# A new written-out order for a linear-attention and token-mixing kernel on one core, from a plan in which small VectorE products exclude GpSimd and DMA transposes follow each other with more room

## The chip, the cores and the metric

The kernel runs on one core of a Trainium2 chip. A core has a matrix engine (TensorE, PE in the profile, with a queue of its own for loading weights, PEld), three engines for elementwise work (VectorE or DVE, ScalarE or ACT, GpSimd or POOL) and SyncE (SP), which here only starts DMA transfers. GpSimd can start transfers too, and does so for those that change the type. Each engine works through its own list of instructions in the order in which the program gives them; engines wait for each other through semaphores. The metric is the time of one execution on the device in microseconds (us); the median of several executions is the time of a kernel.

## What is computed

```python
# attention: B, H, S, D = 4, 8, 768, 48; state is D x D per batch and head
for t in range(S):
    cur = einsum('bhd,bhe->bhde', u * k[t], v[t])
    y[t] = einsum('bhd,bhde->bhe', r[t], state + cur)
    state = w * state + einsum('bhd,bhe->bhde', k[t], v[t])
x = y with its heads side by side                      # (4, 768, 384)
# mixing
theta = x @ w_theta
yr = einsum('ts,bsd->btd', w_tok_r, x * cos(theta))
yi = einsum('ts,bsd->btd', w_tok_i, x * sin(theta))
u = x + yr + yi
out = u + maximum(u @ w_ch, 0)
```

Inputs and output are float32; the kernel works in bfloat16 between.

## The kernel before

**Tiling.** The 768 steps of a batch are cut into chunks of 128, and two chunks make a pair: 3 pairs for each of 4 batches, 12 pairs, numbered 0 to 11. Pairs 0 to 6 take their loads with two neighbouring steps in one row; the later ones take chunks one behind the other. Within a chunk the recurrence becomes matrix products: K and R are multiplied by powers of the decay `w` (`Kw`, `Rw`, L552 and L554, on VectorE or GpSimd), transposed on TensorE against an identity (L491) and copied out of PSUM to `KT` and `RT` (L501 on ScalarE, L502 on VectorE). Scores are products of the two (L603), and VectorE multiplies them by a triangular 0/1 mask into `mAT` (L612). `PD` is the product of `RT` and `KT` (L619); from it comes a diagonal `dg` (L636, L641), which makes the bonus term `yd` with v in bfloat16, `vb` (L645; vb L579 to L583). The state is carried by the tiles `F`, `T`, `N`, `Sb`, `Sd` (L684 to L725). TensorE sums the outputs (L745 states, L758, L774 bonus, which uses the 0/1 tile `place`), and `x` is copied out (L782, L784).

For the mixing, x is transposed to `xT`, on TensorE for some pairs and by a DMA transpose for pairs 5 to 10; theta is a product (L833), cosine and sine run on ScalarE (L840, L844), and `z` is x times both (L848, VectorE). For each of the six chunk rows of a batch three mix tasks of four matmuls each (L870) sum over all 768 steps of a batch and so need the z of all its pairs. `un` adds x (L888, VectorE, into `uu_all`); it is transposed by a DMA transpose on SP's queue for all pairs but the last; the channel product (L903) reads the result; ScalarE applies the maximum (L910), GpSimd adds (L913), SP writes out (L930). The last two pairs end on VectorE (L918).

The mixing weights come by casting DMAs from GpSimd's queue into landing places in tiles that are not used yet (L460), are transposed on TensorE and copied out to `WrT` and `WiT`.

**Order.** All of this is recorded first as 746 tasks, in `P.add`, with what each reads and writes. A task has one way of being done, or several (which engine does it), each with an estimated cost in ns and a flag that says whether it keeps GpSimd from working at the same time. Nothing of these costs is used when the program is built: a planner outside the kernel used them, and left its result as five tables. `ORDER` lists the task numbers in the order in which they are issued, and so fixes the order of each engine's list; `WAYS` has one digit per task for the way; `BANKS` gives the PSUM banks in the order of their use; `AFTER` holds pairs (a, b) in which b is made to wait for a, beyond what the data demands; `IDLE` puts matmuls on a zero tile (fillers, into a bank that nobody reads) behind a task of TensorE: task, bank, number. Task numbers that matter below: 13 `thr` (three tiny operations, L344 to L348), 14 `mask` (L352), 15 `mask_c` (L356), 16 `place` (L361), 29 the small loads of w and u, 71, 114, 157 the Kw of pairs 0, 1, 2, 72, 115, 158 their Rw, 76 the copy of pair 0's RT, 84, 127, 170 the PD of pairs 0, 1, 2, 110, 153, 191 their z, 87 and 130 the yd of pairs 0 and 1, 120 the vb of pair 1, 60 a weight cast, 405 SP's load behind v of pair 1 (its place is read by 120), 355, 490, 506, 674 transposes of `un`.

SP's list at the start is k0, w, k1, r1, r0, the small w/u loads, v0, r2, k2, v1, and then the load that overwrites v1 and so waits for task 120.

Of the kernel before, what the change touches and what calls it, by code (L numbers as in the profile page):

```python
# [20 lines left out]
PE, DVE, ACT, POOL, SP = "PE", "DVE", "ACT", "POOL", "SP"  # L21
# [13 lines left out]


ORDER = [
# [39 lines left out]
]  # L77

WAYS = ("000000000000000000000000000000000000000000100001000010100100000010010000000010000000000000"
    "000001000000000000000000110000000000000000000000100000100000000000010000010000001000000000"  # L80
    "001010000000000010100000000000000010001000000000000000000001000020000000000001000100000000"
    "100000000000001000000000000000000000000000000000000000000000000000000000000000000000000000"
    "000000100001000000000000110010000001000000000000000010000000001000001010000000000000000000"
    "100000100000010000000000000000000000000000000000000000000000000000000000000000000000000010"
    "010000000001011001000000000000000000000100200000000000010000000000000000000001100002000000"
    "100100000000100000000000000000000000000000000000000000000000000000000000000000000000000000"
    "00000000000000000100001000")

BANKS = ("012345670123467523576034610573142716427403274167056732451734214526371675032145723041520715"
    "423527561407524163705701256372056240563513406142350674607534710524713601734654262645240376"  # L90
    "17641632540716306456324157063425176450317")

AFTER = [
# [5 lines left out]
]  # L99


IDLE = [
    (5, 1, 22), (7, 3, 10), (73, 4, 18), (75, 7, 18), (85, 7, 6), (78, 2, 4),
]


# [68 lines left out]
def kernel(  # L175
# [13 lines left out]
    nc = tc.nc  # L189
# [12 lines left out]
    P = Plan()  # L202
# [13 lines left out]
    place = sb.tile([C, 2, C], BF16, name="place")  # L216
# [3 lines left out]
    col_i = sb.tile([C, C], mybir.dt.int32, name="col_i")  # L220
    thr = sb.tile([C, 3], F32, name="thr")
    pi2 = sb.tile([C, 1], F32, name="pi2")
    wu = sb.tile([2 * HP, 2, Dp], F32, name="wu")
    tok_i = sb.tile([C, 1], mybir.dt.int32, name="tok_i")
    tok_f = sb.tile([C, 9], F32, name="tok_f")
# [68 lines left out]
    def setup():  # L294
        if WARM:
            P.add((DVE, 120, False, lambda: nc.vector.memset(zero, 0.0)), wr=["zero"],  # L296
                  prio=-3e4, name="zero")
        P.add((DVE, 250, False, lambda: nc.vector.memset(w_row, 0.0)), wr=["w_row"],
              prio=-2.9e4, name="w zero")
        P.add(sp(lambda: nc.sync.dma_start(out=w_row[:1], in_=rows_of(w, 1)), 400), wr=["w_row"],  # L300
              prio=-1e4, desc=(0, 1, 65), name="w_row", kind="small")
        P.add((DVE, 160, False, lambda: nc.vector.memset(ones, 1.0)), wr=["ones"], prio=-2.8e4,
              name="ones")
        P.add((DVE, 60, False, lambda: nc.vector.memset(pi2, math.pi / 2.0)), wr=["pi2"],
              prio=-210, name="pi2")
        if WARM:
            P.add(pe(WARM_NS[0], lambda: unread(P.bank_of["warm0"], WARM[0], 4)), rd=["zero"],
# [3 lines left out]
            rd=["w_row", "ones"], wr=["spread"], acq=["w"],  # L311
            prio=-1e4, mode=4, name="spread")
        if WARM:
            P.add(pe(WARM_NS[1], lambda: unread(P.bank_of["warm1"], WARM[1], 4)),
                  rd=["zero", "spread"], acq=["warm1"], prio=-1.1e3, name="warm")
# [5 lines left out]
              wr=["tok_i"], prio=-211, name="tok_i")  # L321
        P.add(pool(250, lambda: nc.gpsimd.iota(col_i, pattern=[[1, C]], base=0,
                                               channel_multiplier=0)),
              wr=["col_i"], prio=-210, name="col_i")
# [11 lines left out]
        def identities():  # L336
# [4 lines left out]
              name="ident")  # L341

        def thresholds():
# [2 lines left out]
            nc.vector.scalar_tensor_tensor(thr[:, :1], tok_f[:, 4:5], 2.0, thr[:, 2:],  # L346
                                           op0=Alu.mult, op1=Alu.add)
            return a, nc.vector.tensor_scalar_add(thr[:, 1:2], thr[:, :1], 1.0)  # L348
        P.add((DVE, 440, False, thresholds), rd=["tok_f"], wr=["thr"], prio=-203, name="thr")

        def masks():
            ins = [nc.vector.tensor_scalar(mask01[:, j], col_i, thr[:, j:j + 1], None,  # L352
                                           op0=Alu.is_gt) for j in range(2)]
            return tuple(ins)
        P.add((DVE, 400, False, masks), rd=["thr", "col_i"], wr=["mask"], prio=-201, name="mask")
        P.add((DVE, 200, False, lambda: nc.vector.tensor_scalar(  # L356
            mask_c, col_i, tok_f[:, 4:5], None, op0=Alu.is_gt)), rd=["tok_f", "col_i"],
            wr=["mask_c"], prio=-130, name="mask_c")

        def places():  # L360
            ins = [nc.vector.tensor_scalar(place[:, j], col_i, thr[:, j:j + 1], None,  # L361
                                           op0=Alu.is_equal) for j in range(2)]
            return tuple(ins)
        P.add((DVE, 400, False, places), rd=["thr", "col_i"], wr=["place"], prio=-140,
              name="place")
        P.add((DVE, 160, False, lambda: nc.vector.memset(wu, 0.5)), wr=["wu"], prio=-150,
              name="wu0")
# [606 lines left out]
```

## Time and profile before

| | us |
|---|---|
| median of three runs | 143.26 |
| lowest and highest | 142.03, 143.28 |
| the profiled execution | 142.16 |
| its span, first to last instruction | 140.4 |

| engine | busy us | share of the span |
|---|---|---|
| TensorE | 127.9 | 91% |
| VectorE | 110.9 | 79% |
| ScalarE | 76.1 | 54% |
| GpSimd | 75.0 | 53% |

The profile is one execution. Its views used below are: the busy time by stage; the timeline of an engine, whose rows give the start, the length, engine, line, operation, output and inputs, shapes, the count, and in square brackets the idle time before and what ended it; the chain of waits, followed back from the last instruction, with start and length of each piece; groups of equal instructions with busy time, mean ns of one, and idle time before them; and the table of who waited for whom. The span is first to last instruction, and the device time is a little longer. The granted TensorE clock was 0.994 of full speed.

### The profile page before, as it was taken

The page shows a single profiled execution, that of the slowest core. Times are in us where ns is not written, and L with a number is a line of the kernel's source. Part 1 is how long each engine was busy: PE and PEld are TensorE (multiplying, and loading weights), DVE is VectorE, ACT ScalarE, POOL GpSimd, SP SyncE. Part 2 cuts the span into 40 slices and gives each one's busy share as a digit, 9 for nine tenths or more (in the row PEclk, how much of TensorE's full clock was granted, in tenths as well). Part 3 has the DMA queues.
Part 4 walks back from the last instruction along what each step waited for, and adds up shares of the span by engine and source line. Part 5 has one row for each costly group of instructions (what it writes and reads, how often), then busy time and mean ns, then how long its engine had stood idle before and what let it go on. Part 6 is the DMA issues. An engine that isn't in the chain of part 4 may idle for free.

```text
span 140.4 us, 4622 instructions
## 1 busy us (share of the span) xinstructions
PE 127.9 (91%) x1937; PEld 86.6 (62%) x1937; DVE 110.9 (79%) x202; ACT 76.1 (54%) x149; POOL 75.0 (53%) x83
## 2 busy tenths in 40 slices
PE   5989588999999999979999999898999998999970
PEld 2757466776667776746566665665667775565630
DVE  7049999889889999988975899799689998254280
ACT  3077788598956695377765226751620738910200
POOL 5027669787074639509139966170668984800220
PEclk9999999999999999999999999999999999999997
DMA  4999599899999982799999799999999995432244
GB/s 103 268 257 260 82 204 147 191 244 221 240 278 234 283 190 20 127 161 164 270 249 198 146 181 130 254 155 176 244 215 287 114 99 141 158 117 56 56 168 168
DMA packets 67199, 25.47 MB, mean 181 GB/s; under 512 B 61801, under 2 KB 67178, under 8 KB 67178
## 3 DMA queue, kind: packets, MB, share of 16 engines
q1 hardware_dynamic: 64746, 22.23, 78.4%
q0 software_dynamic: 2432, 2.95, 13.4%
q8 instruction: 15, 0.25, 0.8%
q14 instruction: 6, 0.05, 0.2%
HBM read 20.06 MB, written 4.72 MB: 177 GB/s over the span
## 4 chain that ended last, share of the span: by engine, by line
PE 42%; DMA 24%; DVE 14%; POOL 11%; issue 3%; ACT 2%; SPq 1%; DVEq 0%; POOLq 0%; ACTq 0%
PE bank L870 21%; DMA uu_all<-uu_all 11%; PE bank L491 6%; DMA fin_all<-in_moe_w_tok_r_dram 5%; PE bank L903 5%; DMA ld<-in_r_dram 5%; PE bank L833 4%; DMA xT<-x 4%; DVE mAT L612 3%; POOL Kw L554 2%; DVE Rw L552 2%; POOL yd L645 2%; PE bank L603 2%; POOL PD L619 2%; DVE PD L619 2%
## 5 line engine op out<-in xcount | busy, mean ns | idle before, releaser
L870 PE MATMUL bank<-z,WrT 128*128 128x384 bf16 x144 | 46.9, 326 | 0.0
L870 PE MATMUL bank<-z,WiT 128*128 128x384 bf16 x144 | 46.8, 326 | 0.0
L913 POOL TENSOR_TENSOR fin_all<-fin_all,uu_all 128x384 f32<-128x384 f32 x20 | 17.9, 912 | 25.8 <-ACT fin_all L910 22.4
L888 DVE TENSOR_TENSOR uu_all<-bank,x 128x384 bf16<-128x384 f32 x24 | 12.9, 551 | 8.1 <-PE bank L870 6.6
L870 PEld LDWEIGHTS <-WrT 128*128 128x128 bf16 x144 | 14.1, 98 | 8.2 <-DVE z L848 0.3
L645 POOL TENSOR_TENSOR yd<-dg,vb 128x768 bf16<-128x768 f32 x10 | 14.7, 1472 | 7.8 <-DVE z L848 4.3
L870 PEld LDWEIGHTS <-WiT 128*128 128x128 bf16 x144 | 14.1, 98 | 7.6
L612 DVE TENSOR_TENSOR mAT<-bank,mask 128x512 bf16<-128x512 f32 x28 | 18.1, 680 | 0.3 <-PE bank L603 0.3
L910 ACT ACTIVATE fin_all<-bank 128x384 f32<-128x384 f32 x20 | 9.4, 492 | 16.3 <-issue 8.4
L903 PE MATMUL bank<-Wch,uu_all 128*128 128x384 bf16 x72 | 14.3, 326 | 2.4 <-DMA uu_all<-uu_all 2.4
L840 ACT ACTIVATE trig<-bank,pi 128x384 f16<-128x384 f32 x24 | 13.8, 590 | 3.4 <-PE bank L833 3.2
L501 ACT ACTIVATE RT<-bank 128x1024 bf16<-128x1024 bf16 x10 | 10.2, 1025 | 9.8 <-PE bank L491 9.7
L833 PE MATMUL bank<-Wth,xT 128*128 128x384 bf16 x72 | 14.5, 326 | 0.2 <-DMA xT<-x 0.2
L848 DVE TENSOR_TENSOR z<-x,trig 128x1536 bf16<-128x1536 bf16 x12 | 11.6, 965 | 3.1 <-ACT trig L844 3.0
L612 DVE TENSOR_TENSOR mAT<-bank,mask_c 128x512 bf16<-128x512 f32 x20 | 13.2, 680 | 0.4 <-PE bank L603 0.4
L844 ACT ACTIVATE trig<-bank 128x384 f16<-128x384 f32 x24 | 11.5, 497 | 2.0 <-PE bank L833 2.0
L289 PE MATMUL bank<-zero 128*128 128x128 bf16 (+1 forms) x92 | 10.3, 274 | 1.5 <-DVE zero L296 1.5
L552 POOL TENSOR_TENSOR Rw<-ld,rpow 128x768 bf16<-128x768 f32 x4 | 7.3, 1814 | 7.2 <-DVE z L848 6.3
L903 PEld LDWEIGHTS <-uu_all 128*128 128x128 bf16 x72 | 6.2, 97 | 7.1 <-DMA uu_all<-uu_all 3.4
L552 POOL TENSOR_TENSOR Kw<-ld,kpow 128x768 bf16<-128x768 f32 x3 | 5.4, 1809 | 9.4 <-DVE Kw L552 7.0
L603 PE MATMUL bank<-RT,KT 64*64 64x128 bf16 (+1 forms) x304 | 8.7, 219 | 1.8 <-DVE RT L502 1.3
L552 DVE TENSOR_TENSOR Rw<-ld,rpow 128x768 bf16<-128x768 f32 x8 | 9.2, 1152 | 1.4 <-DMA ld<-in_r_dram 1.4
(115 smaller groups left out, 232.0 us busy)
## 6 DMA issues: line engine op xcount, KB each, us to landing
ld<-in_r_dram SPq DMA_DIRECT2D x12, 384.0 KB, 5.8
out_dram<-fin_all SPq DMA_DIRECT2D x11, 384.0 KB, 2.8
ld<-in_k_dram SPq DMA_DIRECT2D x7, 384.0 KB, 4.9
ld<-in_v_dram SPq DMA_DIRECT2D x7, 384.0 KB, 7.0
ld<-in_k_dram SPq DMA_DIRECT2D x10, 192.0 KB, 4.7
ld<-in_v_dram SPq DMA_DIRECT2D x10, 192.0 KB, 5.6
fin_all<-in_moe_w_tok_i_dram POOLq DMA_DIRECT2D x1, 384.0 KB, 4.8
uu_all<-in_moe_w_tok_r_dram POOLq DMA_DIRECT2D x1, 384.0 KB, 5.8
```

The source lines that it names most:

```text
L552: return eng.tensor_mul(to.rearrange("p j h d -> p h j d")[:, :, :, :D], tokens(i), pw)
L603: ins.append(nc.tensor.matmul(to[:, hp * C:(hp + 1) * C], a, m, start=(hp == 0), stop=(hp == HP - 1), skip_group_check=True))
L612: mask01[:, j] if pairs else mask_c): nc.vector.tensor_mul(
L645: return eng.tensor_mul(yd.rearrange("p a b d -> p (a b) d"), wide(dg, D), vb.rearrange("p a b d -> p (a b) d"))
L833: ins = [nc.tensor.matmul(bank(th)[:, :HD], xT[:, t, dk, :], Wth[:, dk, :], start=(dk == 0), stop=(dk == ND - 1)) for dk in range(ND)]
L840: P.add(act(HD, lambda th=th, t=t, trig=trig: nc.scalar.activation(trig[:, t, 0], bank(th)[:, :HD], Act.Sin, bias=pi2), 144), use=[th], rd ...
L844: P.add(act(HD, lambda th=th, t=t, trig=trig: nc.scalar.activation(trig[:, t, 1], bank(th)[:, :HD], Act.Sin)), use=[th], rd=["sin"], wr=[( ...
L848: P.add(dve(4 * HD, lambda trig=trig, pr=pr: nc.vector.tensor_mul(z[:, 2 * pr:2 * pr + 2], bc(x[:, 2 * pr:2 * pr + 2], 2, 2), trig), 2.0, ...
L870: ins.append(nc.tensor.matmul(bank(tm)[:, :HD], (WrT, WiT)[ri][:, so, to * C:(to + 1) * C], z[:, so, ri], start=(part == 0 and i == 0), st ...
L888: P.add(dve(HD, lambda tm=tm, t=t, to=to, un=un: nc.vector.tensor_add(un[:, t], bank(tm)[:, :HD], x[:, to])), use=[tm], rd=[("x", xi, pr, ...
L903: ins = [nc.tensor.matmul(bank(tf)[:, :HD], uT[:, t, dk, :], Wch[:, dk, :], start=(dk == 0), stop=(dk == ND - 1)) for dk in range(ND)]
L913: P.add(pool(900, lambda t=t, un=un, fin=fin: nc.gpsimd.tensor_add(fin[:, t], fin[:, t], un[:, t])), rd=[("un", j, t)], wr=[("fin", j, t)] ...
```

## The change

Three things change. The planner's notes on five small VectorE tasks get the flag "excludes GpSimd" and other costs (these lines change nothing in the built program). The DMA transposes have more room in the plan; no line of the kernel shows that, and their number and their queue stay. And the tables `ORDER`, `WAYS`, `BANKS`, `AFTER` and `IDLE` are those of a new search.

```diff
 ORDER = [
-    1, 8, 10, 36, 17, 9, 20, 18, 0, 2, 19, 5, 111, 11, 21, 112, 12, 3, 37, 29, 6, 38, 7, 22, 155,
-    23, 24, 25, 154, 71, 26, 114, 73, 113, 74, 72, 116, 30, 117, 13, 115, 75, 31, 35, 77, 76, 28,
+    17, 8, 21, 36, 1, 3, 10, 2, 0, 18, 19, 20, 5, 37, 29, 9, 11, 12, 112, 13, 111, 38, 6, 154, 22,
+    30, 23, 7, 31, 24, 26, 155, 71, 25, 27, 16, 73, 72, 113, 74, 114, 75, 76, 14, 116, 35, 115, 32,
...
 AFTER = [
-    (71, 114), (72, 115), (127, 157), (163, 173), (110, 196), (191, 239), (238, 214), (238, 211),
...
-    (36, 45), (112, 50), (111, 55), (38, 65), (154, 70),
+    (14, 115), (158, 87), (158, 127), (170, 134), (170, 133), (163, 173), (191, 239), (238, 214),
...
+    (112, 39), (37, 40), (155, 45), (38, 50), (154, 60), (193, 65), (278, 70),
 ]
...
 IDLE = [
-    (5, 1, 22), (7, 3, 10), (73, 4, 18), (75, 7, 18), (85, 7, 6), (78, 2, 4),
+    (5, 1, 21), (6, 2, 6), (7, 4, 3), (73, 5, 12), (75, 6, 5), (116, 7, 5), (78, 4, 11),
+    (88, 6, 4), (124, 1, 3), (96, 7, 9), (107, 6, 7), (51, 6, 3),
 ]
...
-        P.add((DVE, 60, False, lambda: nc.vector.memset(pi2, math.pi / 2.0)), wr=["pi2"],
+        P.add((DVE, 60, True, lambda: nc.vector.memset(pi2, math.pi / 2.0)), wr=["pi2"],
...
-        P.add((DVE, 440, False, thresholds), rd=["tok_f"], wr=["thr"], prio=-203, name="thr")
+        P.add((DVE, 520, True, thresholds), rd=["tok_f"], wr=["thr"], prio=-203, name="thr")
...
-        P.add((DVE, 400, False, masks), rd=["thr", "col_i"], wr=["mask"], prio=-201, name="mask")
-        P.add((DVE, 200, False, lambda: nc.vector.tensor_scalar(
+        P.add((DVE, 470, True, masks), rd=["thr", "col_i"], wr=["mask"], prio=-201, name="mask")
+        P.add((DVE, 240, True, lambda: nc.vector.tensor_scalar(
...
-        P.add((DVE, 400, False, places), rd=["thr", "col_i"], wr=["place"], prio=-140,
+        P.add((DVE, 450, True, places), rd=["thr", "col_i"], wr=["place"], prio=-140,
```

What the new tables say where it matters below. On VectorE, `thr` stands right behind the identities, then Kw 0, place, Rw 0, Kw 1, mask. In all, 50 tasks go to another engine. Among those of the first 40 us: Kw of pairs 1 and 2, PD of pair 2, yd of pair 1 and Rw of pair 3 (196) go from GpSimd to VectorE; PD of pair 1 goes from VectorE to GpSimd; the copy of pair 0's RT goes from VectorE to ScalarE, and so do three of the weight copies (47, 52, 64), while two go the other way (59, 62). vb of pair 1 (120) stands on ScalarE behind pair 0's x copies, where it stood ahead of them. SP's list begins k0, w, r0, small w/u, r1, k1, v0, k2, r2, v1, and then the same load that waits for task 120. Rw of pair 2 (158) is now what releases GpSimd's yd of pair 0 and PD of pair 1; a weight cast (65) now waits for r of pair 3 (193). The fillers are 89 instead of 78. Behind transpose 490, TensorE's list has mix 500, mix 504, the transposes of R for pair 9 and an outer product more than before ahead of the first channel product that reads it; behind 674 one channel product more; behind 506 two mixes (686, 687) and a diagonal less, and a group of K transposes and a channel product more.

More of the change, by code (lines that the diff above doesn't have):

```diff
@@ L37 @@
 ORDER = [
[38 rows of a table removed]
[38 rows of a table added]
     724, 740, 727,
 ]
[L79 to L85, printed above, removed]
+WAYS = ("000000000000000000000000000000000000000000100000000000100101001000000000000000000000000000"
+    "000000000000000000000000010000000000010010011001000000100000000000000000010000000000000000"
+    "010010000000000000100000000000010011010000000000000000000001000020000001000000100100000010"
+    "000000000000101000000000000000000000000000000000000000000000000000000000000000000000000000"
+    "000000010000000000000010111000000001000000000000000000000000000000000011000000000000000000"
+    "110000200000010000000000000000000000000000000000000000000000000000000000000000000000000000"
+    "020000000001000010000000000000000000000100200000000000000000000000000000000001100002000000"
     "100100000000100000000000000000000000000000000000000000000000000000000000000000000000000000"
[L87 to L91, printed above, removed]
+    "00000000000000000100000000")
+BANKS = ("012345670134520642157630276145326437640516470627105426157321657635642561720436520514325073"
+    "514156714307142530617426137042137251376062501205713265726314652734105632761450146410416237"
+    "56367450261342507510735240735421736502413")
 AFTER = [
[5 rows of a table removed]
[6 rows of a table added]
 ]
 IDLE = [
-    (5, 1, 22), (7, 3, 10), (73, 4, 18), (75, 7, 18), (85, 7, 6), (78, 2, 4),
+    (5, 1, 21), (6, 2, 6), (7, 4, 3), (73, 5, 12), (75, 6, 5), (116, 7, 5), (78, 4, 11),
+    (88, 6, 4), (124, 1, 3), (96, 7, 9), (107, 6, 7), (51, 6, 3),
 ]
```

79 rows, old and new, of tables (AFTER, ORDER) are left out of this document.

## The prediction

> **What bounds the kernel now.** I read the page's first part, then busy times by stage, then the VectorE and GpSimd timelines of the start, the chain of waits, and last the single waits of TensorE.
>
> ```profile
> span 140.4 us, 4622 instructions
> PE 127.9 (91%) x1937; PEld 86.6 (62%) x1937; DVE 110.9 (79%) x202; ACT 76.1 (54%) x149; POOL 75.0 (53%) x83
> ```
>
> ```profile
> 0.00:37.00 37.00, 31.52 (x572) 22.84 (x573) 29.40 (x66) 25.69 (x48) 21.89 (x30) 1.00 0.98 200
> 37.00:118.00 81.00, 78.29 (x1253) 53.26 (x1251) 72.27 (x122) 44.86 (x91) 47.78 (x47) 1.00 1.05 189
> ```
>
> After its length, a stage row gives the busy time of TensorE, its weight loads, VectorE, ScalarE and GpSimd. From 37 to 118 us TensorE idles for 2.7 us of 81. What it does there is fixed, so a new order can win little more than those 2.7. In the first 37 us it idles for 5.5, and part of its busy time is filler on a zero tile. There VectorE is the full engine, and it is full of something else than work:
>
> ```profile
> 8.58 0.96 DVE L552 TENSOR_TENSOR Kw<-ld,kpow 128x768 bf16<-128x768 f32 x1 [5.11 <-ACT kpow L397]
> 9.75 2.51 DVE L552 TENSOR_TENSOR Rw<-ld,rpow 128x768 bf16<-128x768 f32 x1 [0.21 <-DMA ld<-in_r_dram]
> 12.18 0.14 DVE L344 TENSOR_SCALAR thr<-tok_f 128x1 f32<-128x1 f32 x1
> 12.35 1.81 DVE L346 SCALAR_TENSOR_TENSOR thr<-tok_f,thr 128x1 f32<-128x1 f32 x1
> ...
> 17.56 0.48 DVE L352 TENSOR_SCALAR mask<-col_i,thr 128x128 bf16<-128x128 int32 x2
> ...
> 21.82 1.49 DVE L361 TENSOR_SCALAR place<-col_i,thr 128x128 bf16<-128x128 int32 x2
> ```
>
> ```profile
> 9.62 1.81 POOL L552 TENSOR_TENSOR Kw<-ld,kpow 128x768 bf16<-128x768 f32 x1 [6.96 <-DVE Kw L552]
> 12.33 1.82 POOL L552 TENSOR_TENSOR Rw<-ld,rpow 128x768 bf16<-128x768 f32 x1 [0.89 <-DVE thr L344]
> ...
> 21.27 1.49 POOL L645 TENSOR_TENSOR yd<-dg,vb 128x768 bf16<-128x768 f32 x1
> ```
>
> Set the two fences side by side. VectorE's Rw (0.96 when alone, as Kw shows) takes 2.51 and ends 0.83 after GpSimd's Kw; a threshold on 128 numbers, 0.14 for its sister, takes 1.81 and ends with GpSimd's Rw; the two place products take 1.49 under GpSimd's yd, where the two alike mask products take 0.48. VectorE lost 1.55, 1.67 and 1.01 there: 4.2 us. It sits on the chain of waits (start, length):
>
> ```profile
> 14.21 0.63 PE bank L491 x8
> 14.84 1.22 DVE RT L502
> ...
> 16.10 0.40 PE bank L603 x14
> ...
> 29.31 7.39 DMA fin_all<-in_moe_w_tok_r_dram
> ...
> 37.59 1.30 PE bank L870 x8
> ...
> 69.46 0.49 PE bank L903 x3
> ```
>
> **The start, part by part.** The new order has the thresholds (task 13) done before any GpSimd product runs, and place (16) between Kw and Rw of pair 0. Pair 1's Kw (114) goes from GpSimd to VectorE, and GpSimd's Rw of pair 1 (115) gets an explicit wait for the masks (14). The chain: Kw to 9.54 as now (it waits for ScalarE's powers), place 0.5, Rw 0.96 to 11.0, transposes 0.63, the copy of RT on ScalarE instead of VectorE 1.03, scores near 12.75 instead of 16.10: 3.3 us sooner. Meanwhile VectorE does Kw 1 to 11.95 and the masks to 12.4. GpSimd's Rw 1 so runs from 12.4 to 14.2, as late as today. VectorE's PD product, ready at 13.9, has two inputs in SBUF as Rw has, and the row of 2.51 us says that it waits till 14.2. I take that 0.3; the ends are 0 and the 1.8 of a whole GpSimd product.
>
> The SBUF — State Buffer page of the Trainium skill, section "Who interferes with whom", has a rule that may speak against this part: a VectorE instruction with at most one SBUF input, outside the two-port modes, does not contend with GpSimd. If place is such a one, moving it is worth nothing by that rule, 1.0 us less than by the row, and the wait of 115 for 14 is pure loss. The row of place, 1.49 against 0.48, shows it waiting; the trace decides.
>
> How much of the 3.3 lives on?
>
> ```profile
> 31.57 0.96 DVE L848 TENSOR_TENSOR z<-x,trig 128x1536 bf16<-128x1536 bf16 x1
> ...
> 35.36 0.95 DVE L848 TENSOR_TENSOR z<-x,trig 128x1536 bf16<-128x1536 bf16 x1
> ...
> 38.51 0.95 DVE L848 TENSOR_TENSOR z<-x,trig 128x1536 bf16<-128x1536 bf16 x1
> ```
>
> ```profile
> L612 DVE TENSOR_TENSOR mAT<-bank,mask 128x512 bf16<-128x512 f32 x28 | 18.1, 680 | 0.3 <-PE bank L603 0.3
> L619 DVE TENSOR_TENSOR PD<-RT,KT 128x1024 bf16<-128x1024 bf16 x8 | 5.6, 696 | 0.1
> L645 DVE TENSOR_TENSOR yd<-dg,vb 128x768 bf16<-128x768 f32 x2 | 1.9, 944 | 0.0
> L502 DVE COPY WrT<-bank 128x768 bf16<-128x768 bf16 x4 | 2.2, 550 | 0.0
> L721 DVE TENSOR_TENSOR T<-bank,F 128x192 f32<-128x192 f32 x8 | 2.8, 350 | 0.2
> L840 ACT ACTIVATE trig<-bank,pi 128x384 f16<-128x384 f32 x24 | 13.8, 590 | 3.4 <-PE bank L833 3.2
> L844 ACT ACTIVATE trig<-bank 128x384 f16<-128x384 f32 x24 | 11.5, 497 | 2.0 <-PE bank L833 2.0
> L501 ACT ACTIVATE RT<-bank 128x1024 bf16<-128x1024 bf16 x10 | 10.2, 1025 | 9.8 <-PE bank L491 9.7
> L501 ACT ACTIVATE WiT<-bank 128x768 bf16<-128x768 bf16 x3 | 2.4, 815 | 0.2 <-PE bank L491 0.2
> L579 ACT ACTIVATE vb<-ld 128x768 bf16<-128x768 f32 x6 | 5.0, 838 | 0.0
> L782 ACT ACTIVATE x<-bank 128x384 bf16<-128x384 f32 x11 | 5.0, 495 | 4.9 <-PE bank L774 4.8
> ```
>
> Ahead of the first z product VectorE has, in the new order, 12 score masks of 0.68, 6 Kw or Rw of 0.96, 2 PD of 0.70, a yd of 0.94, 3 weight copies of 0.55, place, masks and uw (1.3 together), 5 state sums of 0.35, an x and a vb of about 0.55: 22 us. Each starts some 0.08 before its forerunner's end (12.18 against 9.75 + 2.51), which leaves 19. From 8.58 that is 28, and today's first z starts at 31.57. But two others are late next:
>
> ```profile
> SPq L446 <- ACT vb L579: 7.6, 1, 7.6
> ld<-in_r_dram SPq DMA_DIRECT2D x12, 384.0 KB, 5.8
> ```
>
> SP's next load waits 7.6 us for ScalarE's vb of pair 1, which now stands behind pair 0's x copies. VectorE reaches the end of Rw 2 near 17.8; that releases GpSimd's yd (1.49), then come the bonus matmuls (about 0.6) and two x copies: 20.9, and vb to 21.7 instead of 23.2. All loads behind it move up by some 1.4, no more. Pair 3's r, 5.8 us to landing, then holds its Rw, which the new order puts on VectorE ahead of z. And ScalarE takes over RT and weight copies; I get its cosines and sines of pair 0 to an end near 30.1 (31.3 today). So the first z comes at about 31.3, 0.3 sooner, with one group of transposes (0.63) more already done. Up to the second z ScalarE still has two sines, two cosines, two weight copies, an x and an RT, 5.3 us or some 4.9 overlapped: 35.0; the third comes near 37.8. The cast whose landing ends TensorE's wait at 36.7 goes out some 1.4 sooner, since GpSimd has lost work ahead of it; with that stall gone, pair 1's z is late in its place. **I take 1.0 us for the start**; the ends are 3.3 and a loss of 2.2 (ScalarE, below).
>
> On SP, r0 and the two small w/u loads pass r1 and k1. k1 isn't needed before 11.0 and today's fourth load is there by 9.75: free. The casts' new waits are for early loads, or for r of pair 3 while GpSimd is idle behind it: nothing. Eleven more fillers stand in gaps: nothing, or 0.7 where TensorE isn't idle:
>
> ```profile
> 10.13 1.17 PE L289 MATMUL bank<-zero 128*128 128x128 bf16 x18
> ```
>
> **The DMA transposes.** All still go through SP's one queue; their places and TensorE's work behind them change.
>
> ```profile
> 61.55 0.82 PE L903 MATMUL bank<-Wch,uu_all 128*128 128x384 bf16 x4 [0.71 <-DMA uu_all<-uu_all]
> ...
> 88.18 0.66 PE L903 MATMUL bank<-Wch,uu_all 128*128 128x384 bf16 x3 [0.68 <-DMA uu_all<-uu_all]
> ...
> 97.01 0.66 PE L903 MATMUL bank<-Wch,uu_all 128*128 128x384 bf16 x3 [0.55 <-DMA uu_all<-uu_all]
> ...
> 116.93 0.66 PE L903 MATMUL bank<-Wch,uu_all 128*128 128x384 bf16 x3 [0.49 <-DMA uu_all<-uu_all]
> ```
>
> For each I compared TensorE's tasks between the last mix that feeds the transpose and the first channel product that reads it. Turn 490 (88.18) gains two mixes of 0.65 (1.30 for two), a transposing group and more, 1.9 or over: its 0.68 goes. Turn 674 (116.93) gains a channel product, 0.49: its 0.49 about goes. Turn 506 (97.01) loses about 0.5 on balance: its wait stays or doubles. Turn 355 (61.55) hangs on a VectorE sum at the same place: stays. **I take 1.1 us**; the ends are 2.4 (all four) and a loss of 0.5. Past the start ScalarE's extra copies (7.5 us over the whole kernel, of 64 idle) are hidden: its rows idle for TensorE.
>
> **The sum.** The profiled execution took 142.16, 1.8 more than its span: 142.16 - 1.0 - 1.1 = 140.1. It lies 1.1 below the median of the runs, 143.26; the same 2.1 off the median is 141.2.
>
> **Rivals.** *All of the start lives on*: z near 28, loads in time. For it: VectorE was the full engine; against it: SP's 7.6 us. 143.26 - 3.3 - 1.1 = 138.9. *It doesn't do what it says*: collisions go, but the loads keep z where it was, and transposes on one queue land as before: 143.26 - 0.3 = 143.0. *ScalarE takes VectorE's place between 30 and 38 us*: up to the third z it gains RT, three weight copies and small ones against two weight copies and small ones, net 1.5; this decides if the second z starts later than 35.36. Then all mixing comes 1.5 later, and the 0.7 of fillers stands before work: 143.26 + 2.2 = 145.5. For it: it works in order and is busy 25.69 of 37; against it: that leaves 11 idle.
>
> **Chances.** Forecast 0.45, all of the start 0.14, nothing 0.18, ScalarE late 0.23. One per cent, 1.43 us, is about what a measurement of this kernel can tell from no change. The forecast's own range is 139.8 to 142.6; 0.34 of its 0.45 lies below 141.8. So faster 0.34 + 0.14 = 0.48, within 0.11 + 0.18 = 0.29, slower 0.23. The range 138.7 to 145.3 takes in the first rival and about half of the last.
>
> **What would show it.** Thresholds and place without a stretched one, no Rw of 2.5 us; scores of pair 0 near 12.8; the load behind ScalarE's vb near 21.7; z products near 31.3, 35.0 and 37.8; no channel product waiting near 88 and 117. A second z after 35.4, transposed K and R that wait for ScalarE while TensorE idles, or over 3 us of TensorE idle from 37 to 118 would make it wrong.

## The result and the profile after

| us | before | after |
|---|---|---|
| median, runs side by side on one chip | 142.06 | 140.38 |
| lowest and highest of 20 runs each | 140.63, 143.57 | 139.17, 142.53 |
| profiled execution, its span | 142.16, 140.4 | 140.2, 138.4 |

The ratio of after to before is 0.9878, 95% interval 0.9843 to 0.9913: faster by 1.2%. The prediction's 141.2 against the 143.26 that it started from is a ratio of 0.9856, inside that interval. The runs of one kernel spread by 2 to 3 us, so single profiles are read below for where time goes, and the repeated runs for how much. Ratios and their intervals, here and below, take in only those runs of a kernel that lie within 1.5% of its fastest, while the medians take in all, so a ratio isn't the quotient of two medians.

The page after, first the span and the busy time of each engine:

```profile
span 138.4 us, 4633 instructions
...
PE 129.0 (93%) x1948; PEld 87.6 (63%) x1948; DVE 106.6 (77%) x197; ACT 81.6 (59%) x158; POOL 70.1 (51%) x79
```

The two stages (length, then busy time of TensorE, weight loads, VectorE, ScalarE, GpSimd):

```profile
0.00:37.00 37.00, 33.33 (x592) 24.44 (x593) 28.41 (x69) 27.06 (x49) 15.42 (x27) 1.00 1.00 211
37.00:118.00 81.00, 79.59 (x1259) 53.89 (x1258) 70.53 (x116) 49.46 (x99) 49.82 (x47) 1.00 0.95 188
```

Between 37 and 118 us TensorE now idles for 1.4 us where it idled for 2.7. VectorE's busy time fell by 4.3 us over the whole kernel, ScalarE's rose by 5.5, GpSimd's fell by 4.9. The table of who waited for whom, TensorE's rows:

```profile
PE bank L291 <- DVE zero L298: 1.7, 1, 1.7
PE bank L835 <- issue: 1.2, 1, 1.2
PE bank L671 <- issue: 1.0, 1, 1.0
PE bank L493 <- DVE Kw L554: 0.3, 1, 0.3
```

There is no row for a channel product that waits for its DMA transpose. Before, the four waits shown with the prediction made the largest row, 2.4 us; now all four are gone, where the prediction counted on two. Two rows are new: TensorE stood still for 1.2 and 1.0 us, and "issue" says that nothing the profile records released it.

The start on VectorE, in order:

```profile
9.10 0.96 DVE L554 TENSOR_TENSOR Kw<-ld,kpow 128x768 bf16<-128x768 f32 x1 [1.02 <-ACT kpow L399]
9.97 0.48 DVE L363 TENSOR_SCALAR place<-col_i,thr 128x128 bf16<-128x128 int32 x2
10.36 0.95 DVE L554 TENSOR_TENSOR Rw<-ld,rpow 128x768 bf16<-128x768 f32 x1
11.23 0.95 DVE L554 TENSOR_TENSOR Kw<-ld,kpow 128x768 bf16<-128x768 f32 x1
12.10 0.48 DVE L354 TENSOR_SCALAR mask<-col_i,thr 128x128 bf16<-128x128 int32 x2
...
14.23 0.87 DVE L621 TENSOR_TENSOR PD<-RT,KT 128x1024 bf16<-128x1024 bf16 x1
```

Rw takes 0.95 where it took 2.51, and the two place products 0.48 where they took 1.49: these collisions with GpSimd are gone, as the prediction took them from the old rows. The rule weighed there (the Trainium skill, "SBUF — State Buffer", section "Who interferes with whom") would have left place as slow as it was, if place is a product outside the two-port modes; it got 1.0 us quicker for two. Whether it runs in such a mode no run here shows. The scores of pair 0 follow on TensorE at 13.15 us, 2.95 sooner than before (16.10). The three z products:

```profile
32.02 0.95 DVE L850 TENSOR_TENSOR z<-x,trig 128x1536 bf16<-128x1536 bf16 x1
...
34.77 0.95 DVE L850 TENSOR_TENSOR z<-x,trig 128x1536 bf16<-128x1536 bf16 x1
...
37.97 0.95 DVE L850 TENSOR_TENSOR z<-x,trig 128x1536 bf16<-128x1536 bf16 x1
```

They stand 0.45 later, 0.59 and 0.54 sooner than before. So nearly 3 us of lead at 13 us have become half a microsecond at 35, and the span ends 2.0 sooner: most of the time must be won elsewhere. Half a microsecond is little to read from single profiles: in the other profiles of kernels with the old start unchanged, the first z stands anywhere from 30.79 to 31.62 us.

### The profile page after: what moved, and what is told of

It is laid out like the page before. It is cut to its first block, busy times and chain, and to the rows that moved or that the text cites. A ratio compares the mean times of both kernels' runs of the same rounds, so it can differ in the third digit from the quotient of the medians.

```text
span 138.4 us, 4633 instructions
## 1 busy us (share of the span) xinstructions
PE 129.0 (93%) x1948; PEld 87.6 (63%) x1948; DVE 106.6 (77%) x197; ACT 81.6 (59%) x158; POOL 70.1 (51%) x79
## 3 DMA queue, kind: packets, MB, share of 16 engines
q0 software_dynamic: 2432, 2.95, 13.0%
## 4 chain that ended last, share of the span: by engine, by line
PE 75%; DVE 9%; ACT 4%; DMA 3%; issue 3%; POOL 1%; SPq 1%; DVEq 0%; POOLq 0%
PE bank L872 29%; PE bank L493 10%; PE bank L835 8%; PE bank L905 7%; PE bank L291 4%; PE bank L605 4%; DMA ld<-in_r_dram 3%; PE bank L671 3%; PE bank L760 2%; DVE Rw L554 2%; PE bank L812 2%; PE bank L776 2%; PE bank L638 2%; DVE mAT L614 1%; POOL Rw L554 1%
## 5 line engine op out<-in xcount | busy, mean ns | idle before, releaser
L554 POOL TENSOR_TENSOR Rw<-ld,rpow 128x768 bf16<-128x768 f32 x6 | 10.9, 1816 | 18.3 <-DVE mask L354 10.1
L291 PE MATMUL bank<-zero 128*128 128x128 bf16 (+1 forms) x103 | 12.3, 275 | 1.7 <-DVE zero L298 1.7
L503 ACT ACTIVATE RT<-bank 128x1024 bf16<-128x1024 bf16 x12 | 12.4, 1030 | 2.1 <-PE bank L493 2.0
L291 PEld LDWEIGHTS <-zero 128*128 128x128 bf16 x103 | 8.0, 111 | 5.0 <-issue 1.9
L503 ACT ACTIVATE KT<-bank 128x1024 bf16<-128x1024 bf16 x9 | 9.2, 1021 | 2.8 <-PE bank L493 2.8
L647 POOL TENSOR_TENSOR yd<-dg,vb 128x768 bf16<-128x768 f32 x7 | 10.3, 1475 | 0.8 <-DVE Rw L554 0.6
L554 DVE TENSOR_TENSOR Rw<-ld,rpow 128x768 bf16<-128x768 f32 x6 | 7.6, 1261 | 2.2 <-DMA ld<-in_r_dram 2.2
```

The costliest lines, as they stand in the source:

```text
L291: ins = [nc.tensor.matmul(bank_t[k][:, :wide * C].rearrange("p (a c) -> p a c", a=wide), zero, bc(zero, 1, wide), start=True, stop=True, s ...
L503: P.add([act(n * C, lambda: nc.scalar.activation(dst, src(), Act.Copy)), dve(n * C, lambda: nc.vector.tensor_copy(dst, src()), 1.0 if pair ...
L554: return eng.tensor_mul(to.rearrange("p j h d -> p h j d")[:, :, :, :D], tokens(i), pw)
```

## The experiments

Two theories stood at the beginning. By theory A the gain is shared as the prediction had it, 1.0 us in the start and 1.1 at the transposes; by theory B all of it is won behind 36 us. In all the kernels the whole computation is left in; only tables differ. "New" and "old" in the short diffs are the tables after and before. A kernel made of the two takes the first tasks of one order and then all the rest in the sequence of the other; each task keeps the engine that it has in the order it is taken from, and the waits of `AFTER` go with it.

**The start alone, and the rest alone.**

```diff
-ORDER = old
+ORDER = new[:186] + [s for s in old if s not in new[:186]]   # new up to 36 us
```

> The first 186 tasks of the changed order (up to about 36 us), the rest in the old order. Theory A (the prediction's split: start 1.0, transposes 1.1): 1.0 us faster than the kernel before, ratio 0.993. Theory B (the start's lead, 2.7 us at 15 us in the changed trace, is used up by the first z product, and the whole gain comes from the channel products that no longer wait for DMA transposes): within 0.4 us of before, ratio 0.997 to 1.003, and the four waits of 0.5 to 0.7 us of channel products are back.

```diff
-ORDER = old
+ORDER = old[:186] + [s for s in new if s not in old[:186]]   # new from 36 us on
```

> The first 186 tasks in the old order, the rest in the changed one. Theory A: about 1.0 us faster than before, ratio 0.993. Theory B: the whole gain of the change, 1.7 us, ratio 0.988, with the three Rw, threshold and place stalls of VectorE (4.2 us) still there and no channel product waiting.

The start alone gave 0.9969 (0.9923 to 1.0016), the rest alone 0.9878 (0.9838 to 0.9919). The rest by itself is worth what the whole change is worth, as theory B has it. Its stage row, and TensorE's two largest waits in it, both of the first 13 us:

```profile
37.00:118.00 81.00, 80.35 (x1262) 54.28 (x1262) 70.86 (x117) 50.05 (x100) 51.36 (x48) 1.00 1.00 189
```

```profile
PE bank L283 <- DVE zero L290: 1.5, 1, 1.5
PE bank L485 <- POOL Kw L546: 1.0, 1, 1.0
```

From 37 to 118 us TensorE idles for 0.65 us: the four waits on transposes are gone, and nothing stands in their place. One thing in it was not as expected: of the three stalls of VectorE in the old start the first, at Rw, isn't there in this profile (0.96 us, not 2.51), and its first z stands at 30.79 us, 0.78 sooner than in the kernel before with the same order. So a part of this profile's lead isn't the rest's, and only its waits are read. The start alone kept one of them (0.6 us), and got two of 0.7 us on the transposes of x.

**Only later channel products.** The kernel before, with six channel products one to three TensorE tasks later, so that the transposes have time to land.

```diff
-ORDER = old
+ORDER = old with 356 and 359 behind 376, 491 behind 504, 507 behind 478, 675 and 678 behind 691
```

> The kernel before, in which only the channel products that waited for a DMA transpose stand one to three TensorE tasks later (six of them). Theory B, if cover behind the transposes is all it needs: the four waits (2.4 us in all) go and the kernel is 1.5 to 2.4 us faster, ratio 0.983 to 0.989. Rival: what stands behind them waits in their place (z products or VectorE sums are the next to be late): under 0.5 us faster, ratio over 0.996.

1.0028 (0.9993 to 1.0063): no gain. The four waits are gone, and others stand in TensorE's table:

```profile
PE bank L826 <- DMA xT<-x: 1.3, 1, 1.3
...
PE bank L484 <- DMA z<-in_moe_w_tok_i_dram: 0.7, 1, 0.7
PE bank L484 <- ACT fin_all L903: 0.6, 1, 0.6
```

TensorE comes to other tasks whose data are not there either: a transpose of x (1.35 us, at 99.06) and ScalarE's step behind a channel product that is now later (0.58, at 64.33), 1.9 us where 2.4 went. The wait for a weight cast, 0.7, is at 39.62 us, ahead of everything that was moved, and so belongs to this execution and not to the change. Room behind a transpose brings nothing here if everything else stays.

**The small products alone.** The kernel before, with thresholds, masks and place directly behind the identities, ahead of any GpSimd product.

```diff
 ORDER = [
-    ... 111, 11, 21, 112, 12, 3, 37, ...
+    ... 111, 11, 21, 112, 12, 13, 14, 16, 15, 3, 37, ...
```

> The kernel before, in which thresholds, masks, place and the causal mask stand right behind the identities on VectorE, where it idles for 5 us; nothing else is moved, the stretched Rw of 2.5 us stays. VectorE saves 4 us of blocked and own time in the start. Theory B (loads and ScalarE end the lead): scores of pair 0 earlier by about 1.9 us, but under 0.5 us faster in all, ratio over 0.996. Rival (VectorE sets the start): 1.5 us faster or more, ratio under 0.990.

0.9966 (0.9923 to 1.0009). The scores of pair 0 stand at 14.19 us, 1.91 sooner, as expected; the time, as with the new start, is 0.3% less at the middle and not told from nothing.

**Where in the rest.** The new order from 63 us on, from 105 us on, and between the two only.

```diff
-ORDER = old
+ORDER = old[:343] + [s for s in new if s not in old[:343]]   # from 63 us on
+ORDER = old[:603] + [s for s in new if s not in old[:603]]   # from 105 us on
+ORDER = the first of these up to its 603rd task, then the sequence of old   # 63 to 105 us
```

> The kernel before up to about 63 us, the new order behind it. The old start with the new rest from 36 us on gave 0.9878. Theory C: the gain lies behind 63 us, at the transposes of 82 to 97 us and of 110 to 117 us whose channel products no longer wait (0.68, 0.55 and 0.49 us of wait in the kernel before, 1.7 us together): ratio 0.985 to 0.991, and no wait of a channel product on a transpose behind 63 us. Rival D, that the stretch from 36 to 63 us carries it (its lead there in one profile was the 0.8 us with which it came out of the start): ratio above 0.996.

> The kernel before up to about 105 us, the new order behind it. Theory C: only the last waiting transpose (0.49 us of wait) and the work around it are changed: ratio 0.994 to 0.998, 0.3 to 0.8 us. Rival D': the last third carries most: ratio below 0.992. Rival: nothing of it here: 0.999 to 1.002.

> The kernel before with the new order between about 63 and 105 us alone: two of the waiting transposes lie there (0.68 and 0.55 us of wait). Theory C: both waits are gone and the rest follows: ratio 0.989 to 0.994, 0.8 to 1.5 us. Rival: what is won there is waited for behind it, as with the channel products that were only put later: ratio 0.998 to 1.002. With the run from 105 us on this should add up to the run from 63 us on.

They gave 0.9947 (0.9901 to 0.9992), 1.0109 (1.0069 to 1.0150) and 1.0067 (1.0025 to 1.0109). The first is a smaller gain than was expected, the others are losses, and they do not add up: the expectations failed. The likely cause, not tested by itself, is the seam: at 105 us the two orders have different tasks done, and a kernel that changes over there must catch up. TensorE's longest waits, in the kernel from 105 us on and in the one between:

```profile
108.55 0.62 PE L484 MATMUL bank<-ident,Kw 128*128 128x128 bf16 x8 [1.23 <-DVE F L710]
```

```profile
108.61 0.62 PE L484 MATMUL bank<-ident,Rw 128*128 128x128 bf16 x8 [1.05 <-POOL Rw L545]
```

Both stand just behind the seam; neither whole kernel stops there. These runs so don't share the gain out over the stretches; that stays open.

**Less room in the new order.** The changed kernel with the transposes 490 and 506 behind the loads that stand next in SP's queue, with their channel products in place.

```diff
-ORDER = new
+ORDER = new with 490 behind 534 (load v), 506 behind 572 and 571 (loads of k)
```

> The changed kernel with two of its DMA transposes, those issued at 82.73 and 88.71 us, put behind the loads that stand next in SP's queue, so some 2.4 and 2.3 us later; their channel products at 88.45 and 94.11 us keep their places. Theory: room is what counts, and a wait of TensorE on a transpose is paid in full: about 1.5 us of wait at each comes back, and the time rises by 2 to 3 us, ratio to the kernel before 1.002 to 1.010. Rival: TensorE is behind other work anyway, and the waits take the place of others: 0.988 to 0.995.

1.0009 (0.9969 to 1.0050), 1.3% above the changed kernel's 0.9878: 1.9 us, below the 2 to 3 expected. Only one wait came back. SP's row of the second transpose and TensorE's row of the product that reads it:

```profile
89.32 1.46 SPq L503 DMA_TRANSPOSE uu_all<-uu_all  x1
```

```profile
94.55 1.15 PE L898 MATMUL bank<-Wch,uu_all 128*128 128x384 bf16 x6 [1.47 <-DMA uu_all<-uu_all]
```

The first transpose went out at 82.45 us (82.73 in the changed kernel), since the load ahead of it was quickly issued; its product stood 5.29 us behind it instead of 5.72, and didn't wait. The second cost a wait of 1.47 us, and it is paid; the rest of the 1.9 isn't accounted for. Room is needed, then, but by itself it brings nothing: the first half of that from this run, the second from the later channel products.

**Three products between the engines.** In the rest, tasks 366 (a Kw), 382 (a yd) and 422 (a PD) went from GpSimd to VectorE. Once they are put back in the kernel of old start and new rest, once moved alone in the kernel before.

```diff
-WAYS = old start, new rest
+WAYS = the same, with 366, 382, 422 on GpSimd
```

> Old start and new rest from 36 us on (0.9878 before), with the products 366, 382 and 422 of the rest put back from VectorE to GpSimd, where the kernel before had them (1.81 us, 1.47 us and 2.12 us there, 0.95, 0.95 and 0.83 us on VectorE). Theory F: these three are what lets the rest run ahead of the transposes, and the gain of 1.7 us falls to 0.5 us or less: ratio 0.996 to 1.003, with TensorE waiting for GpSimd near 60 or 75 us. Theory C: the order and the room behind the transposes carry the gain, the engine of three products does not: ratio 0.986 to 0.992.

```diff
-WAYS = old
+WAYS = old, with 366, 382, 422 on VectorE
```

> The kernel before, order and start unchanged, with the products 366, 382 and 422 alone put from GpSimd (1.81, 1.47 and 2.12 us) to VectorE (0.95, 0.95 and 0.83 us). Theory F1: the engine of the three is the gain by itself, whatever the order: ratio 0.985 to 0.992. Theory F2: engine and order only gain together, because in the old order TensorE waits for none of the three (its waits behind 36 us are the channel products' on the transposes): ratio 0.997 to 1.004, with the waits of the channel products still there.

Put back: 0.9987 (0.9945 to 1.0030), no gain left that can be told from nothing. Moved alone: 1.0151 (1.0096 to 1.0205), 1.5% slower, outside what either theory expected. (Both profiled executions lie 1.4 and 1.7 us above their kernel's median, so waits are read from them, not the total.) GpSimd's timeline in the first, and TensorE's row behind it:

```profile
73.77 2.12 POOL L613 TENSOR_TENSOR PD<-RT,KT 128x1024 bf16<-128x1024 bf16 x1 [0.20 <-ACT RT L495]
75.84 1.48 POOL L639 TENSOR_TENSOR yd<-dg,vb 128x768 bf16<-128x768 f32 x1
...
79.14 1.83 POOL L548 TENSOR_TENSOR Kw<-ld,kpow_c 128x768 bf16<-128x768 f32 x1
80.91 2.54 POOL L546 TENSOR_TENSOR Rw<-ld,rpow 128x768 bf16<-128x768 f32 x1
```

```profile
83.50 0.62 PE L485 MATMUL bank<-ident,Rw 128*128 128x128 bf16 x8 [1.21 <-POOL Rw L546]
```

PD and yd, 3.6 us of GpSimd, push the Kw and Rw behind them, and TensorE waits 1.21 us for that Rw. In the kernel before, VectorE made it, at 72.42 us; the new order gives it (task 451) to GpSimd, in exchange for PD and yd, so that this run undoes one half of an exchange. Task 366 makes TensorE wait in the same way near 57 us, for 0.52 us. The other run does one half of it alone. VectorE then has no good place for the PD:

```profile
78.44 1.74 DVE L612 TENSOR_TENSOR PD<-RT,KT 128x1024 bf16<-128x1024 bf16 x1
```

```profile
77.82 1.81 POOL L547 TENSOR_TENSOR Kw<-ld,kpow_c 128x768 bf16<-128x768 f32 x1
```

```profile
80.84 0.43 PE L662 MATMUL bank<-vb,Kw 128*64 128x48 bf16 x16 [1.05 <-DVE mAT L605]
```

It runs into GpSimd's Kw (to 79.63 us) and takes 1.74 instead of the 0.83 that it takes in the changed kernel, where GpSimd has nothing beside it but the last 0.28 us of a cast; the score mask behind it is late, and TensorE waits 1.05. A collision as in the old start comes back here. It isn't the largest wait of this profile: at 69.67 us TensorE waits 1.77 for a transposed x, and whether the three products are behind that too isn't shown. Nor were the waits moved along that hold GpSimd back in the new order: (366, 261), (366, 297), (382, 326) and (382, 329) of `AFTER`. So neither the order with these three on the old engine nor the engine with the old order has the gain: it needs both. Which of the other 30 tasks of the rest that change their engine matter, no run tried.

**No fillers.** The changed kernel without its 89 fillers, to see what the two "issue" gaps belong to.

```diff
-IDLE = [(5, 1, 21), (6, 2, 6), ... (51, 6, 3)]
+IDLE = []
```

> The changed kernel without its 89 filler matmuls, which compute nothing that is used. In two profiles of kernels with the new start TensorE stood still in front of its matmuls number 350 and 861 (1.02 and 1.19 us, and 1.30 and 0.49 us), and nothing that the profile shows released it. Theory E: the gaps belong to the place in TensorE's own list of instructions, not to the work there: without the fillers number 350 is other work, reached some 3 us later, so the gap of 1.0 us in the outer product near 22.3 us goes, any gap that is left stands in front of number 350 or 861 again, and the time falls by 0.5 to 1.5 us against the changed kernel: ratio to the kernel before 0.977 to 0.985. Rival: the gaps belong to the work (outer product, theta product): they stay there, ratio 0.986 to 0.990. Rival: the fillers are needed, the granted clock falls in the first 20 us and the time rises: above 0.995.

0.9867 (0.9786 to 0.9949): not told from the changed kernel, and not the gain of 0.5 to 1.5 us that was expected; its six runs spread from 139.17 to 143.86. The granted clock was 0.999 in the profiled execution, but 0.962 and 0.971 in two of the others, where the changed kernel with its fillers had 0.981 or more in 20 runs. Whether the fillers are needed for the clock stays open. The gap at 22 us is gone and the first z stands at 30.23 us instead of 32.02. But a longer gap appears elsewhere, at other work:

```profile
46.30 0.32 PE L863 MATMUL bank<-z,WrT 128*128 128x384 bf16 x1 [1.67 <-issue]
```

What that says is told in the last section.

**The best of both.** The old start with the small products early, and the new rest.

```diff
-ORDER = old
+ORDER = (old[:186] with 13, 14, 16, 15 behind 12) + [s for s in new if s not in old[:186]]
```

> Old start with the four small products of the set-up (thresholds, two masks, place) directly behind the identities, and the new rest from 36 us on. The two parts gave 0.9966 and 0.9878 by themselves. If they add: ratio 0.980 to 0.987, about 139.2 us. If what the start wins is waited for at the loads near 36 us, as in the changed kernel: 0.986 to 0.991.

0.9826 (0.9783 to 0.9869), a median of 139.18 us, with all its runs between 138.86 and 139.63. That fits two parts that add (0.9966 times 0.9878 is 0.9844). It is faster than the kernel before; against the changed kernel the intervals overlap, so that it is the faster of the two is likely, not shown.

## Why the prediction came out right, and where its steps did not

**What bounds it.** That a new order can win little more than TensorE's 2.7 us of idle time between 37 and 118 us held: 1.4 are left, and 0.65 with the old start. The chain of waits, followed back from the end, by engine, before and after:

```profile
PE 42%; DMA 24%; DVE 14%; POOL 11%; issue 3%; ACT 2%; SPq 1%; DVEq 0%; POOLq 0%; ACTq 0%
```

```profile
PE 75%; DVE 9%; ACT 4%; DMA 3%; issue 3%; POOL 1%; SPq 1%; DVEq 0%; POOLq 0%
```

DMA has nearly left it, and TensorE's own work is three quarters.

**The start, 1.0 us.** The stretched products went as written, and the chain behind them came nearly on time: scores at 13.15 (12.8 predicted), the load behind ScalarE's vb at 21.85 (21.7), the second and third z at 34.77 and 37.97 (35.0 and 37.8). The first z was 0.7 later than the 31.3 predicted. The reason given for the loss of lead, SP's loads behind vb, isn't what the trace shows: no Rw waits for its r there. Nor was it ScalarE, which had the cosines and sines of pair 0 done at 30.29 (30.1 predicted). VectorE came to the z only at 32.02, behind the Rw of pair 3, after it had stood idle for 1.9 us since 23 us. TensorE's row shows a stop there:

```profile
23.33 0.24 PE L671 MATMUL bank<-vb,Kw 64*64 64x48 bf16 x4 [1.02 <-issue]
```

and VectorE's yd of pair 1, two steps behind it, waits:

```profile
24.11 0.96 DVE L647 TENSOR_TENSOR yd<-dg,vb 128x768 bf16<-128x768 f32 x1 [1.09 <-ACT dg L643]
```

In the run without fillers this stop is gone and the first z stands at 30.23; that the stop is what cost the lead is argued from this, since the fillers went too. The time of the start alone is 0.3% of 142, 0.4 us, with an interval from a gain of 1.1 to a loss of 0.2. The term of 1.0 is not refuted, but it is near the upper end of what was measured.

**The DMA transposes, 1.1 us.** Here the prediction was too small. The mechanism was right, a product that no longer waits, but "Turn 506 loses about 0.5 on balance: its wait stays or doubles" and "Turn 355 ... stays" failed. The step took the landing time and VectorE's sum as given and counted TensorE's tasks only. That count held: from the end of the last mix that feeds turn 506 to the product TensorE has 6.52 us of work before (89.94 to 96.46) and 5.79 after (87.83 to 93.62): 0.73 less, about the 0.5 that was forecast. What it left out is, first, the sum `un` on VectorE, before and then after:

```profile
89.66 0.95 DVE L848 TENSOR_TENSOR z<-x,trig 128x1536 bf16<-128x1536 bf16 x1
90.70 0.36 DVE L703 TENSOR_TENSOR Sb<-bank,N 128x192 bf16<-128x192 f32 x1
90.98 0.55 DVE L888 TENSOR_TENSOR uu_all<-bank,x 128x384 bf16<-128x384 f32 x1
```

```profile
87.87 0.56 DVE L890 TENSOR_TENSOR uu_all<-bank,x 128x384 bf16<-128x384 f32 x1 [0.84 <-PE bank L872]
```

Before, the sum stood behind a z product and began 1.04 us after the mix; now it begins 0.04 after it. That 1.0 us more than makes up for TensorE's 0.73 less of work. Second, SP's queue, before and then after:

```profile
87.73 0.53 SPq L930 DMA_DIRECT2D out_dram<-fin_all  x1
88.31 0.46 SPq L446 DMA_DIRECT2D ld<-in_v_dram  x1
88.82 0.96 SPq L446 DMA_DIRECT2D ld<-in_k_dram  x1
89.83 0.94 SPq L446 DMA_DIRECT2D ld<-in_v_dram  x1
91.55 1.22 SPq L508 DMA_TRANSPOSE uu_all<-uu_all  x1
```

```profile
87.58 0.53 SPq L932 DMA_DIRECT2D out_dram<-fin_all  x1
88.15 0.46 SPq L448 DMA_DIRECT2D ld<-in_v_dram  x1
88.71 1.62 SPq L510 DMA_TRANSPOSE uu_all<-uu_all  x1
```

Before, the transpose went out behind three loads, and its product, which began as soon as it had landed, began at 97.01, 5.46 us later. Now it goes out 0.28 us after the sum, behind one load; the first product that reads it begins at 93.62, 4.91 us later, and doesn't wait. In the experiment with less room the same transpose, behind three loads again, took 5.23. With 5.46 a wait of 0.55 would still be there, so the sooner sum and the shorter landing are both needed. That the loads ahead in the queue are what lengthens a transpose isn't shown: turn 490 took 5.16 us behind one load before, and in the changed kernel and the one with less room it landed 5.2 us after its issue behind two loads and 4.8 behind three. For turn 355 the product stands 4.40 us behind the transpose where it stood 4.56; from the end of VectorE's sum to the product TensorE needs 4.43 us, and needed 3.87 without its wait: 0.56 more of other work, in the place that the prediction took for unchanged.

All four waits are 2.43 us in the profile; the rest alone was worth 1.2% of 141.89, 1.7 us (1.1 to 2.3). Nor is this gain one of room alone, as the prediction had it: later channel products brought nothing, and three products that the prediction passed over, a Kw, a yd and a PD at 55 and 72 us, decide whether it is there at all.

**The sum** was right in part by luck, because two errors met: 1.0 and 1.1 were forecast, 0.4 and 1.7 measured for the parts alone, with intervals whose ends just reach the forecast. The changed kernel, with 1.7 in all, has a little less than their sum; its gap of 1.19 us near 50 us, which the old start with the new rest doesn't have, would account for that, but the intervals are too wide to show it.

**The rivals.** That all of the start lives on (138.9) fell with the first z at 32.02 and with the start alone, which by its interval is worth 1.1 us at most. That the change does nothing (143.0) fell with the ratio; its first half, collisions gone and z where it was, is what the trace shows, its second half, transposes landing as before, is wrong. That ScalarE takes VectorE's place (145.5) would have needed a second z behind 35.36; it stood at 34.77.

## What to carry to other kernels

A wait on the bounding engine is worth its length only if the work behind it is ready sooner too: test it by moving the waiting task alone. When two orders are compared, follow the whole path to a waiting task, here mix, sum, transpose and product, and not only the work that the waiting engine does meanwhile; the landing time of a transfer isn't fixed either. And the engine of a product and its place belong together: in this kernel VectorE made a PD in 0.83 us in its new place, and took 1.74 for it where GpSimd was working beside it.

## What the hardware showed that was not expected

TensorE seems to run out of instructions at times. The page's DMA queues include one of kind "instruction"; with columns packets, MB and share, its row in the changed kernel and in the one without fillers:

```profile
q8 instruction: 15, 0.25, 0.7%
```

```profile
q8 instruction: 14, 0.23, 0.7%
```

That is 16,384 bytes for each packet. The changed kernel has 1948 matmuls and as many weight loads, 3896 for 15 packets, and the other 3718 for 14: about 260 to a packet. The trace has one such packet at 20.98 us (0.94 long) and one at 48.18 (1.19), each while the data queues are full, and TensorE stops at 22.31 and at 49.85, in front of its matmuls number 350 and 861 (counted from 0), and goes on 1.4 and 1.7 us behind the packet's end. In the kernel with less room it stops in front of the same two numbers, for 1.30 and 0.49 us. Without fillers it stops in front of number 733, 1.3 us behind the end of a packet that began at 44.07 us (0.96 long). 861 - 733 is 128, and 861 - 350 is 511, four times 128 less one: all lie on one grid of 128 matmuls with their weight loads. So the expectation that a gap stands at 350 or 861 again failed by its words, and the grid holds. Through the first 1500 matmuls of the changed kernel one packet begins between each crossing of this grid and the next, and the two that begin latest, 37 and 21 matmuls ahead of the next crossing, are those behind which TensorE stops. The Trainium skill, "Runtime: NRT & Kernel Launch", section "Instruction fetch mechanics", says that instructions are refilled in blocks of 16 KiB, 256 instructions, and that the cost is mostly hidden. The size agrees with the packets here; mostly hidden agrees too, with two of 15 blocks seen, but those two cost 1.02 and 1.19 us. That the fetch is the cause is argued from this grid and from the times of the packets; no run delayed a fetch by itself. It would explain why the gap at 350 is there where the start is fast: the kernel before reaches number 350 at 24.71 us, with its packet at 21.67, and doesn't stop; it comes there 2.1 us behind that packet's end.
